# Decode attention on one Trainium2 core: 19 heads on VectorE, 13 on TensorE, wo of 24 heads and the MLP as one row, and wo of two heads by four DMA engines

## The chip, the cores and the metric

The kernel runs on one core of one Trainium2 chip. The metric is the device time of one execution in microseconds (us); lower is better. The first quotation for the kernel before is a median of 198.81 us over 3 runs (197.66 to 199.92). The profile is one execution; its span (196.6 us for the kernel before) leaves out about 2 us of start and end that the measured time includes.

In what follows PE is TensorE (matmuls), PEld its weight loads, DVE is VectorE, ACT is ScalarE, POOL is GpSimd and SP is SyncE, which issues most of the transfers.

## The reference, cut to what matters

One token of 512 features is normalised, attends with 32 heads to the last 4,096 of 32,768 cached positions, and is gated by an MLP.

```python
W = min(4096, max(256, Sk // 4))                       # 4096 of 32768
q = (xn @ wq) ...                                      # 32 heads x 128
scores = einsum("bhqd,bhkd->bhqk", q, k[:, :, Sk-W:]) * Dh**-0.5
o = einsum("bhqk,bhkd->bhqd", softmax(scores), v[:, :, Sk-W:])
s = o.reshape(B, Sq, Hq*Dh) @ wo                       # 4096 x 512
g = silu(B_ref(xn, w1, w2, w3, w4))                    # MLP, 512 -> 1376 -> 512
return x + s * g
```

The keys of one head in the window are 1 MB of bf16, the values too. With 64 such MB of keys and values, 4 MB each of wq and wo and the MLP weights, 78.85 million bytes have to come in.

## The kernel before: the parts that the argument touches

Transfers go out in one fixed order, on one queue: MLP weights, wq, the keys of head 0 to 4, then keys of head i and values of head i-5 in turn. There are 12 buffers for keys (wo of 8 heads takes one of them, three times) and 7 for values.

```python
def k_head(h, kn):                         # scores of one head
    ...
    if h % 2 == 0:                         # 16 heads on VectorE
        nc.vector.tensor_tensor(out=prod[:], in0=kn[:],
            in1=q_bc[:, h // 2:h // 2 + 1, :].to_broadcast([P, NC, Dh]), op=ALU.mult)
        nc.vector.tensor_reduce(out=s["sS"][:, hl // 2, :], in_=prod[:], axis=AX.X, op=ALU.add)
    else:                                  # 16 heads on TensorE, ScalarE copies
        for b in range(NB):
            for i in range(8):
                nc.tensor.transpose(pt[:, i, :], kn[:, b * 8 + i, :], ident_bf[:])
            nc.scalar.copy(out=kt[:, b * 8:(b + 1) * 8, :], in_=pt[:])
            if b == 0:
                flush()                    # matmuls of the head before
        pending.append((s["sT"], hl, h, kt))
    if hl == G - 1:                        # every 4th head
        softmax(g)                         # needs sS (VectorE) and sT (TensorE)

def rows_add(ps, col, w, last):            # "narrow": 4 matmuls of 128 columns,
    for j in range(KC):                    # accumulated in PSUM, no VectorE work
        nc.tensor.matmul(ps[32 * j:32 * j + 1, :], lhsT=col, rhs=w[0:k, j * P:(j + 1) * P],
                         start=False, stop=last, skip_group_check=True)

def apply_wo(i, ox):                       # wo of block i (8 heads), i = 0, 1, 2 and the few
    for t in range(8):
        rows_add(y_ps, ox[:, t:t + 1], wo_blk[i][:, t, :], False)
...
small.tile([P, 16], BF16, name="pad")      # decides where the later buffers lie
```

`oT` is the product of a head's probabilities `pT` with its values. After every 8 heads VectorE repacks the 8 outputs (`spread`, `pick`, `ox`), and TensorE applies that block of wo. wo of heads 24 to 31 is split: 2.5 heads (`wo_few`) are spread over the partitions so that five DMA engines carry them (in the trace each half of this load has five landings, a load of 128 partitions sixteen), the others come as rows at the end. After the last values come the last rows of wo, then `y = y_ps * g_row`, `out_row`, and the write of the output.

## Time and profile before

| kernel before | us | where it is read |
|---|---|---|
| median of 6 runs beside the changed kernel | 197.98 | the runs |
| span of the profiled run | 196.6 | the page |
| last group's softmax (`pT`) starts | 182.53 | ScalarE's row `pT<-e` |
| last values have landed | 191.60 | the chain of waits |
| `y` starts | 193.24 | the chain of waits |

The first profile line is the page's busy time by engine. After it comes VectorE's timeline around the third wo block: start and duration in us, engine, line, operation, output and inputs, shapes, count, and in brackets the idle time before the instruction and what ended it.

```profile
PE 125.2 (64%) x2448; PEld 112.3 (57%) x2448; DVE 129.5 (66%) x165; ACT 69.3 (35%) x82; POOL 6.3 (3%) x13
```

```profile
167.34 0.27 DVE L369 TENSOR_REDUCE ox<-pick 128x8 bf16<-128x64 f32 x1
169.34 2.29 DVE L274 TENSOR_TENSOR prod<-kv,q_bc 128x4096 bf16<-128x4096 bf16 x1 [1.74 <-DMA kv<-in_A_k_cache_dram]
171.67 4.42 DVE L277 TENSOR_REDUCE sS<-prod 128x32 f32<-128x4096 bf16 x1
176.12 0.22 DVE L296 TENSOR_REDUCE m<-sS 128x2 f32<-128x64 f32 x1
179.97 0.22 DVE L297 TENSOR_REDUCE m<-sT 128x2 f32<-128x64 f32 x1 [3.63 <-PE sT L255]
```

VectorE starts head 30 at 169.34, as soon as its keys are there, while TensorE is still at the third block of wo and at head 29. It has finished at 176.1 and then idles 3.63 us until TensorE has the scores of head 31. So here TensorE, not VectorE, sets the last softmax, and VectorE has idle time on both sides of head 30.

### The profile page before, as it was taken

To read this page: it belongs to the slowest core of one execution; us is meant where nothing else is said; L and a number is where in the kernel's file an instruction comes from. 1 tells how busy PE (TensorE), PEld (TensorE's weight loads), DVE (VectorE), ACT (ScalarE), POOL (GpSimd) and SP (SyncE) were. 2 spreads that over 40 slices of the span, in tenths; PEclk is the share of its full clock that TensorE was granted. 3 is DMA by queue.
4 is the path that set the end of the run, shared out by engine and by line. 5 is a ranking of instruction groups with operands and counts; after the bars stand their busy time and mean duration, and the time that the engine had idled before them with its cause. 6 is when DMAs were issued, how large, how long until landed. Compare 5 with 4: busy or idle time off the path is not lost.

```text
span 196.6 us, 5355 instructions
## 1 busy us (share of the span) xinstructions
PE 125.2 (64%) x2448; PEld 112.3 (57%) x2448; DVE 129.5 (66%) x165; ACT 69.3 (35%) x82; POOL 6.3 (3%) x13
## 2 busy tenths in 40 slices
PE   0564497646959683199565672399575930898563
PEld 0453335536949673199465662399574930897452
DVE  1530059998969988785497829693599479681401
ACT  2003028819445270076234340077170700455000
POOL 2110007000000000000000000000000000000000
PEclk9999999957675885557555555555566675555555
DMA  6999899999999999999999999999999999999970
GB/s 197 412 499 423 368 430 417 427 427 418 428 420 425 423 423 423 423 427 425 425 422 428 420 425 422 427 428 422 422 427 422 427 422 430 427 421 388 383 282 7
DMA packets 11480, 79.18 MB, mean 403 GB/s; under 512 B 1402, under 2 KB 2202, under 8 KB 2458
## 3 DMA queue, kind: packets, MB, share of 16 engines
q1 hardware_dynamic: 11306, 78.85, 96.4%
q8 instruction: 19, 0.31, 0.6%
q10 hardware_dynamic: 152, 0.00, 0.0%
q14 instruction: 3, 0.02, 0.0%
HBM read 78.84 MB, written 0.00 MB: 401 GB/s over the span
## 4 chain that ended last, share of the span: by engine, by line
DMA 91%; PE 5%; SPq 1%; issue 0%; DVE 0%
DMA kv<-in_A_v_cache_dram 41%; DMA kv<-in_A_k_cache_dram 31%; DMA wo<-in_A_wo_dram 10%; DMA wq_sb<-in_A_wq_dram 10%; PE qb_ps L234 3%; SPq L76 1%; PE qT_ps L225 1%; PE oT L402 1%; PE y_ps L139 0%; DVE y L454 0%; DVE out_row L456 0%
## 5 line engine op out<-in xcount | busy, mean ns | idle before, releaser
L284 ACT COPY kt<-pt 128x1024 bf16<-128x1024 bf16 x64 | 60.2, 1026 | 67.4 <-PE pt L283 67.4
L277 DVE TENSOR_REDUCE sS<-prod 128x32 f32<-128x4096 bf16 x16 | 70.6, 4415 | 0.3
L283 PE MATMUL pt<-ident_bf,kv 128*128 128x128 bf16 x512 | 53.0, 294 | 5.2 <-DMA kv<-in_A_k_cache_dram 4.5
L283 PEld LDWEIGHTS <-kv 128*128 128x128 bf16 x512 | 48.8, 138 | 6.8 <-DMA kv<-in_A_k_cache_dram 4.8
L274 DVE TENSOR_TENSOR prod<-kv,q_bc 128x4096 bf16<-128x4096 bf16 x16 | 36.6, 2285 | 7.5 <-DMA kv<-in_A_k_cache_dram 5.3
L402 PEld LDWEIGHTS <-kv 128*128 128x128 bf16 x1024 | 30.4, 102 | 16.3 <-issue 9.4
L402 PE MATMUL oT<-pT,kv 128*128 128x1 bf16 x1024 | 32.6, 165 | 8.0 <-DMA kv<-in_A_v_cache_dram 4.3
L255 PE MATMUL sT<-qT_bf,kt 128*128 128x1 bf16 x512 | 20.4, 166 | 3.8 <-ACT kt L284 3.4
L255 PEld LDWEIGHTS <-kt 128*128 128x128 bf16 x512 | 18.3, 103 | 4.8 <-ACT kt L284 4.6
L297 DVE TENSOR_REDUCE m<-sT 128x2 f32<-128x64 f32 x8 | 1.8, 224 | 18.4 <-PE sT L255 18.4
L139 PEld LDWEIGHTS <-ox 128*1 128x1 bf16 x96 | 2.2, 115 | 19.5 <-DVE ox L369 19.5
L363 PE MATMUL ox_ps<-spread,to 128*128 128x64 bf16 x4 | 0.8, 211 | 17.4 <-DVE spread L360 17.4
L316 ACT ACTIVATE pT<-e 128x128 bf16<-128x128 f32 x8 | 2.5, 310 | 20.4 <-DVE e L312 20.3
L307 PEld LDWEIGHTS mb_ps<-md,ones_f 4*128 4x128 f32 x16 | 3.5, 266 | 6.1 <-DVE md L304 6.1
L307 PE MATMUL mb_ps<-md,ones_f 4*128 4x4 f32 x16 | 4.2, 328 | 4.4 <-DVE md L304 4.4
L322 PE MATMUL den_ps<-pT,ones_bf 128*128 128x128 bf16 x8 | 2.1, 260 | 7.3 <-ACT pT L316 7.2
L234 PE MATMUL qb_ps<-wq_sb,xn_rep 128*128 128x512 bf16 x16 | 6.3, 578 | 0.0
L236 ACT CAST q_bc<-qb_ps 128x512 bf16<-128x512 f32 x4 | 2.3, 586 | 10.9 <-PE qb_ps L234 10.9
L300 PE MATMUL mt_ps<-ident_f,m 128*4 128x128 f32 x8 | 2.7, 335 | 4.8 <-DVE m L297 4.8
L405 DVE TENSOR_TENSOR o<-oT,rden 128x1 bf16<-128x1 f32 x4 | 0.6, 161 | 7.0 <-PE oT L402 7.0
L225 PE MATMUL qT_ps<-xn_bf,wq_sb 128*128 128x1 bf16 x64 | 1.9, 165 | 5.3 <-DMA wq_sb<-in_A_wq_dram 5.3
L225 PEld LDWEIGHTS <-wq_sb 128*128 128x128 bf16 x64 | 1.8, 104 | 5.6 <-DMA wq_sb<-in_A_wq_dram 5.6
(97 smaller groups left out, 63.3 us busy)
## 6 DMA issues: line engine op xcount, KB each, us to landing
kv<-in_A_k_cache_dram SPq DMA_DIRECT2D x32, 1024.0 KB, 19.6
kv<-in_A_v_cache_dram SPq DMA_DIRECT2D x32, 1024.0 KB, 19.6
wq_sb<-in_A_wq_dram SPq DMA_DIRECT2D x1, 4096.0 KB, 19.2
wo<-in_A_wo_dram SPq DMA_DIRECT2D x3, 1024.0 KB, 19.6
w_sb<-in_B_w_dram SPq DMA_DIRECT2D x1, 1376.0 KB, 6.7
w_sb<-in_B_w_dram SPq DMA_DIRECT2D x1, 1024.0 KB, 8.7
w_sb<-in_B_w_dram SPq DMA_DIRECT2D x1, 512.0 KB
wo_rows<-in_A_wo_dram SPq DMA_DIRECT2D x1, 384.0 KB, 15.9
```

The lines of the kernel that those rows point to most:

```text
L225: nc.tensor.matmul(qT_ps[:, h:h + 1], lhsT=wq_sb[:, c, h * Dh:(h + 1) * Dh], rhs=xn_bf[:, c:c + 1], start=(c == 0), stop=(c == KC - 1))
L234: nc.tensor.matmul(qb_ps[:], lhsT=xn_rep[:, c, :], rhs=wq_h[:, c, 2 * i:2 * i + 8:2, :], start=(c == 0), stop=(c == KC - 1))
L236: nc.scalar.copy(out=q_bc[:, i:i + 4, :], in_=qb_ps[:])
L255: nc.tensor.matmul(sT[:, hl // 2, c:c + 1], lhsT=kt[:, c, :], rhs=qT_bf[:, h:h + 1], start=True, stop=True)
L274: nc.vector.tensor_tensor(out=prod[:], in0=kn[:], in1=q_bc[:, h // 2:h // 2 + 1, :].to_broadcast([P, NC, Dh]), op=ALU.mult)
L277: nc.vector.tensor_reduce(out=s["sS"][:, hl // 2, :], in_=prod[:], axis=AX.X, op=ALU.add)
L283: nc.tensor.transpose(pt[:, i, :], kn[:, b * 8 + i, :], ident_bf[:])
L284: nc.scalar.copy(out=kt[:, b * 8:(b + 1) * 8, :], in_=pt[:])
L300: nc.tensor.transpose(mt_ps[:], m1[:].rearrange("p a b -> p (a b)"), ident_f[:])
L307: nc.tensor.matmul(mb_ps[:], lhsT=ones_f[0:G, :], rhs=md[:], start=True, stop=True)
L316: nc.scalar.activation(out=pT[:], in_=e[:], func=ACT.Exp, scale=scale)
L402: nc.tensor.matmul(oT[:, k:k + 1], lhsT=v[:, c, :], rhs=s["pT"][:, hl % 2, hl // 2, c:c + 1], start=(c == 0), stop=(c == NC - 1))
```

## The change

Its intent is to give TensorE and ScalarE less to do, to shorten the program, and to even out the DMA engines at the end. Three more heads (5, 13, 21) go to VectorE. wo of the first 24 heads and the MLP's output are computed "wide", as one row of 512 columns with one matmul instead of four; VectorE then takes the row out of PSUM and adds it to a running row. `wo_few` shrinks to 2 heads on four engines, and wo of two further heads is loaded ahead of the last values instead of earlier.

```diff
+MORE = (1, 3, 5)                 # groups in which VectorE takes three of four heads
-NE = 5
+NE = 4
-    small.tile([P, 16], BF16, name="pad")
+    small.tile([P, 32], BF16, name="pad")
...                               # MLP: 15 matmuls of 512 columns into hr_ps, copied to hr,
+    rows_add(h2_ps, one_f, hr, True)
...
-        if h % 2 == 0:
+        on_v, on_t = map(at, places(g))
+        if hl in on_v:
...
+    y_row = small.tile([1, D], FP32, name="y_row")
     def apply_wo(i, ox):
+        if i == few_block:
+            for t in range(8):
+                rows_add(y_ps, ox[:, t:t + 1], wo_blk[i][:, t, :], False)
+            return
+        yr_ps = ps_misc.tile([1, D], FP32, tag="misc", name="yr_ps")
         for t in range(8):
-            rows_add(y_ps, ox[:, t:t + 1], wo_blk[i][:, t, :], False)
+            nc.tensor.matmul(yr_ps[:], lhsT=ox[:, t:t + 1], rhs=wo_blk[i][:, t, :], start=(t == 0),
+                             stop=(t == 7))
+        if i == 0:
+            nc.vector.tensor_copy(out=y_row[:], in_=yr_ps[:])
+        else:
+            nc.vector.tensor_tensor(out=y_row[:], in0=y_row[:], in1=yr_ps[:], op=ALU.add)
+        if i == few_block - 1:
+            rows_add(y_ps, one_f, y_row, False)
...
+            if h == H - 1:
+                load_rows(h_part, H - G - h_part)
             v = load_kv(v_pool, A_v_cache, h)
...
-    for h in range(H - G, H):
+    for h in range(h_part, H):
         apply_rows(h)
```

Cut are the indexing that follows from 19 heads (`q_at`, `places`, the order inside a group) and the memsets.

More of the change, by code (lines that the diff above doesn't have):

```diff
@@ L106 @@
     nc.vector.memset(ones_f[:], 1.0)
+    one_f = ones_f[0:1, 0:1]
     ones_bf = const.tile([P, P], BF16, name="ones_bf")
@@ L172 @@
     nc.vector.tensor_copy(out=xn_bf[:], in_=xn_f[:])
-    xn_rep = small.tile([P, KC, P], BF16, name="xn_rep")
+    xn_rep = wts.tile([P, KC, P], BF16, name="xn_rep")
     nc.vector.tensor_copy(out=xn_rep[:], in_=xn_bf[:].unsqueeze(2).to_broadcast([P, KC, P]))
@@ L189 @@
     nc.vector.tensor_scalar(out=z3_bf[:], in0=xc3[:], scalar1=rstd3[:], scalar2=None, op0=ALU.mult)
-    hsr_ps = ps_misc.tile([P, P], FP32, tag="misc", name="hsr_ps")
-    rows_open(hsr_ps)
-    for c in range(KC):
-        rows_add(hsr_ps, shifted_bf[:, c:c + 1], w2_sb[:, c, :], c == KC - 1)
-    x1_row = small.tile([P, P], FP32, name="x1_row")
-    nc.vector.tensor_scalar(out=x1_row[:], in0=x_row[:], scalar1=negmean[:], scalar2=rstd[:],
+    xn_row = small.tile([P, P], FP32, name="xn_row")
+    nc.vector.tensor_scalar(out=xn_row[:], in0=x_row[:], scalar1=negmean[:], scalar2=rstd[:],
                             op0=ALU.add, op1=ALU.mult)
-    nc.vector.tensor_tensor(out=x1_row[:], in0=x1_row[:], in1=hsr_ps[:], op=ALU.add)
     chunks = [(P, slice(r, 8 * P, 8)) for r in range(8)]
@@ L210 @@
     nc.scalar.activation(out=a_bf[0:96, 10:11], in_=a_ps[0:96, 10:11], func=ACT.Gelu_apprx_tanh)
+    hr_ps = ps_misc.tile([1, D], FP32, tag="misc", name="hr_ps")
+    for c in range(KC):
+        nc.tensor.matmul(hr_ps[:], lhsT=shifted_bf[:, c:c + 1], rhs=w2_sb[:, c, :], start=(c == 0),
+                         stop=False)
+    for i, (m, _) in enumerate(chunks):
+        nc.tensor.matmul(hr_ps[:], lhsT=a_bf[0:m, i:i + 1], rhs=w4_sb[0:m, i, :], start=False,
+                         stop=(i == len(chunks) - 1))
@@ L211 @@
+    hr = wts.tile([1, D], FP32, name="hr")
+    nc.vector.tensor_copy(out=hr[:], in_=hr_ps[:])
     h2_ps = ps_misc.tile([P, P], FP32, tag="misc", name="h2_ps")
     rows_open(h2_ps)
-    for i, (m, _) in enumerate(chunks):
-        rows_add(h2_ps, a_bf[0:m, i:i + 1], w4_sb[:, i, :], i == len(chunks) - 1)
+    rows_add(h2_ps, one_f, hr, True)
     bv = small.tile([P, P], FP32, name="bv")
-    nc.vector.tensor_tensor(out=bv[:], in0=x1_row[:], in1=h2_ps[:], op=ALU.add)
+    nc.vector.tensor_tensor(out=bv[:], in0=xn_row[:], in1=h2_ps[:], op=ALU.add)
@@ L217, with places, at @@
     g_row = small.tile([P, P], FP32, name="g_row")
     nc.scalar.activation(out=g_row[:], in_=bv[:], func=ACT.Silu)
-    qT_ps = ps_misc.tile([P, H], FP32, tag="misc", name="qT_ps")
-    for h in range(1, H, 2):
+    def places(g):
+        if g in MORE:
+            return slice(0, G - 1, 1), slice(G - 1, G, 1)
+        return slice(0, G, 2), slice(1, G, 2)
+    def at(sl):
+        return list(range(G)[sl])
+    ve_runs = [range(8 * i, 8 * i + 8, 2) for i in range(H // 8)]
+    ve_runs += [range(G * MORE[0] + 1, G * MORE[-1] + 2, G * (MORE[1] - MORE[0]))]
@@ L224 @@
+    ve_heads = [h for r in ve_runs for h in r]
+    pe_heads = [h for h in range(H) if h not in ve_heads]
+    assert sorted(ve_heads) == [G * g + i for g in range(H // G) for i in at(places(g)[0])]
+    q_at = {h: i for hs in (ve_heads, pe_heads) for i, h in enumerate(hs)}
+    qT_ps = ps_misc.tile([P, len(pe_heads)], FP32, tag="misc", name="qT_ps")
+    for i, h in enumerate(pe_heads):
         for c in range(KC):
-            nc.tensor.matmul(qT_ps[:, h:h + 1], lhsT=wq_sb[:, c, h * Dh:(h + 1) * Dh],
+            nc.tensor.matmul(qT_ps[:, i:i + 1], lhsT=wq_sb[:, c, h * Dh:(h + 1) * Dh],
@@ L226 @@
                              rhs=xn_bf[:, c:c + 1], start=(c == 0), stop=(c == KC - 1))
-    qT_bf = small.tile([P, H], BF16, name="qT_bf")
-    nc.vector.tensor_copy(out=qT_bf[:, 1::2], in_=qT_ps[:, 1::2])
-    q_bc = small.tile([P, H // 2, Dh], BF16, name="q_bc")
+    qT_bf = small.tile([P, len(pe_heads)], BF16, name="qT_bf")
+    nc.vector.tensor_copy(out=qT_bf[:], in_=qT_ps[:])
+    q_bc = small.tile([P, len(ve_heads), Dh], BF16, name="q_bc")
     wq_h = wq_sb[:].rearrange("p c (h d) -> p c h d", d=Dh)
-    for i in range(0, H // 2, 4):
-        qb_ps = ps_tr.tile([P, 4, Dh], FP32, tag="pt", name="qb_ps")
+    for r in ve_runs:
+        n = len(r)
+        qb_ps = ps_tr.tile([P, n, Dh], FP32, tag="pt", name="qb_ps")
@@ L233 @@
         for c in range(KC):
-            nc.tensor.matmul(qb_ps[:], lhsT=xn_rep[:, c, :], rhs=wq_h[:, c, 2 * i:2 * i + 8:2, :],
+            nc.tensor.matmul(qb_ps[:], lhsT=xn_rep[:, c, :], rhs=wq_h[:, c, r[0]:r[-1] + 1:r.step, :],
                              start=(c == 0), stop=(c == KC - 1))
-        nc.scalar.copy(out=q_bc[:, i:i + 4, :], in_=qb_ps[:])
+        nc.scalar.copy(out=q_bc[:, q_at[r[0]]:q_at[r[0]] + n, :], in_=qb_ps[:])
     make_masks(8)
@@ L251, with qk @@
     rows_open(y_ps)
-    def qk(sT, hl, h, kt):
+    def qk(sT, i, h, kt):
         for c in range(NC):
-            nc.tensor.matmul(sT[:, hl // 2, c:c + 1], lhsT=kt[:, c, :], rhs=qT_bf[:, h:h + 1],
+            nc.tensor.matmul(sT[:, i, c:c + 1], lhsT=kt[:, c, :], rhs=qT_bf[:, q_at[h]:q_at[h] + 1],
                              start=True, stop=True)
@@ L268, in k_head @@
                 "sT": ps_s.tile([P, G // 2, NC], FP32, tag="sT", name="sT"),
-                "sS": sm_pool.tile([P, G // 2, NC], FP32, tag="sS", name="sS"),
+                "sS": sm_pool.tile([P, G - 1, NC], FP32, tag="sS", name="sS"),
             }
         s = st[g]
-        if h % 2 == 0:
+        on_v, on_t = map(at, places(g))
+        if hl in on_v:
             prod = prod_pool.tile([P, NC, Dh], BF16, tag="prod", name="prod")
             nc.vector.tensor_tensor(out=prod[:], in0=kn[:],
-                                    in1=q_bc[:, h // 2:h // 2 + 1, :].to_broadcast([P, NC, Dh]),
+                                    in1=q_bc[:, q_at[h]:q_at[h] + 1, :].to_broadcast([P, NC, Dh]),
                                     op=ALU.mult)
-            nc.vector.tensor_reduce(out=s["sS"][:, hl // 2, :], in_=prod[:], axis=AX.X, op=ALU.add)
+            nc.vector.tensor_reduce(out=s["sS"][:, on_v.index(hl), :], in_=prod[:], axis=AX.X, op=ALU.add)
         else:
@@ L286, in k_head @@
                     flush()
-            pending.append((s["sT"], hl, h, kt))
+            pending.append((s["sT"], on_t.index(hl), h, kt))
             if hl == G - 1:
@@ L294, in softmax @@
         s = st[g]
-        m1 = sm_pool.tile([P, 2, G // 2], FP32, tag="m1", name="m1")
-        nc.vector.tensor_reduce(out=m1[:, 0, :], in_=s["sS"][:], axis=AX.X, op=ALU.max)
-        nc.vector.tensor_reduce(out=m1[:, 1, :], in_=s["sT"][:], axis=AX.X, op=ALU.max)
+        parts = [(pl, len(at(pl)), src[:, 0:len(at(pl)), :])
+                 for pl, src in zip(places(g), (s["sS"], s["sT"]))]
+        m1 = sm_pool.tile([P, G], FP32, tag="m1", name="m1")
+        for pl, n, src in parts:
+            nc.vector.tensor_reduce(out=m1[:, pl], in_=src, axis=AX.X, op=ALU.max)
         mt_ps = ps_misc.tile([G, P], FP32, tag="misc", name="mt_ps")
-        nc.tensor.transpose(mt_ps[:], m1[:].rearrange("p a b -> p (a b)"), ident_f[:])
+        nc.tensor.transpose(mt_ps[:], m1[:], ident_f[:])
         mx = sm_pool.tile([G, 1], FP32, tag="mx", name="mx")
@@ L305, in softmax @@
                                 op0=ALU.mult)
-        mb_ps = ps_misc.tile([P, 2, G // 2], FP32, tag="misc", name="mb_ps")
+        mb_ps = ps_misc.tile([P, G], FP32, tag="misc", name="mb_ps")
         nc.tensor.matmul(mb_ps[:], lhsT=ones_f[0:G, :], rhs=md[:], start=True, stop=True)
-        mb = sm_pool.tile([P, 2, G // 2], FP32, tag="mb", name="mb")
+        mb = sm_pool.tile([P, G], FP32, tag="mb", name="mb")
         nc.vector.tensor_copy(out=mb[:], in_=mb_ps[:])
-        e = sm_pool.tile([P, 2, G // 2, NC], FP32, tag="e", name="e")
-        for i, src in enumerate((s["sS"], s["sT"])):
-            nc.vector.tensor_tensor(out=e[:, i], in0=src[:],
-                                    in1=mb[:, i, :].unsqueeze(2).to_broadcast([P, G // 2, NC]),
+        e = sm_pool.tile([P, G, NC], FP32, tag="e", name="e")
+        for pl, n, src in parts:
+            nc.vector.tensor_tensor(out=e[:, pl, :], in0=src,
+                                    in1=mb[:, pl].unsqueeze(2).to_broadcast([P, n, NC]),
                                     op=ALU.subtract)
-        pT = sm_pool.tile([P, 2, G // 2, NC], BF16, tag="pT", name="pT")
+        pT = sm_pool.tile([P, G, NC], BF16, tag="pT", name="pT")
         nc.scalar.activation(out=pT[:], in_=e[:], func=ACT.Exp, scale=scale)
@@ L332 @@
     FEW = 8 * 8 * NE
-    h_part, r_part = divmod(24 * P + FEW, P)
-    assert h_part + 1 < H - G and 0 < r_part < P and r_part % 32 == 0
+    h_part = 8 * few_block + FEW // P
+    assert FEW % P == 0 and h_part < H - G
     o_blk, wo_blk = {}, {}
@@ L398, in v_head @@
                 nc.vector.memset(o_blk[i][:], 0.0)
-        k = 2 * (hl % 2) + hl // 2
         oT, o = s["oT"], o_blk[i]
         for c in range(NC):
-            nc.tensor.matmul(oT[:, k:k + 1], lhsT=v[:, c, :], rhs=s["pT"][:, hl % 2, hl // 2, c:c + 1],
+            nc.tensor.matmul(oT[:, hl:hl + 1], lhsT=v[:, c, :], rhs=s["pT"][:, hl, c:c + 1],
                              start=(c == 0), stop=(c == NC - 1))
         if h >= H - G:
-            nc.vector.tensor_tensor(out=o[:, h % 8:h % 8 + 1], in0=oT[:, k:k + 1],
-                                    in1=s["rden"][:, k:k + 1], op=ALU.mult)
+            nc.vector.tensor_tensor(out=o[:, h % 8:h % 8 + 1], in0=oT[:, hl:hl + 1],
+                                    in1=s["rden"][:, hl:hl + 1], op=ALU.mult)
         elif hl == G - 1:
-            nc.vector.tensor_tensor(
-                out=o[:, h % 8 - 3:h % 8 + 1].rearrange("p (a b) -> p b a", b=2),
-                in0=oT[:].rearrange("p (b a) -> p b a", b=2),
-                in1=s["rden"][:].rearrange("p (b a) -> p b a", b=2), op=ALU.mult)
+            nc.vector.tensor_tensor(out=o[:, h % 8 - 3:h % 8 + 1], in0=oT[:], in1=s["rden"][:],
+                                    op=ALU.mult)
         ready, later[:] = later[:], []
@@ L419, in step @@
                 later.append(lambda: apply_wo(i, ox))
-                if i == few_block:
-                    later.append(lambda: [apply_rows(h) for h in range(h_part, H - G)])
             later.append(step)
@@ L434 @@
             wo_rows = v_pool.tile([P, H - h_part, D], BF16, tag="wo_rows", bufs=1, name="wo_rows")
-            nc.gpsimd.memset(wo_rows[0:r_part, 0, :], 0.0)
         if i >= LAG:
             h = i - LAG
+            if h == H - 1:
+                load_rows(h_part, H - G - h_part)
             v = load_kv(v_pool, A_v_cache, h)
@@ L442 @@
                 load_few()
-            if h == H - G - 1:
-                load(wo_rows[r_part:, 0, :], A_wo[h_part * P + r_part:(h_part + 1) * P, :])
-                load_rows(h_part + 1, H - G - h_part - 1)
             if h == H - 1:
```

## The prediction

> **What bounds the kernel now.** I read the page first: the slices, the queues, the shares of the chain.
>
> ```profile
> DMA  6999899999999999999999999999999999999970
> GB/s 197 412 499 423 368 430 417 427 427 418 428 420 425 423 423 423 423 427 425 425 422 428 420 425 422 427 428 422 422 427 422 427 422 430 427 421 388 383 282 7
> ...
> q1 hardware_dynamic: 11306, 78.85, 96.4%
> q8 instruction: 19, 0.31, 0.6%
> ...
> DMA 91%; PE 5%; SPq 1%; issue 0%; DVE 0%
> ```
>
> The DMA engines are full in every slice up to the last three, at some 424 GB/s. No compute engine is near that (the page gives VectorE 66%, TensorE 64%, ScalarE 35%). 91% of the chain of waits is transfers, and the 78.85 MB have to come in under either kernel. So engine work counts only in two places: where the DMA engines stop being full, and after the last value has landed. The table by windows and the chain in order of time show both:
>
> ```profile
> core 0: us, PE busy (x) PEld busy (x) DVE busy (x) ACT busy (x) POOL busy (x), PEclk, DMA share, GB/s
> ...
> 160.00:170.00 10.00, 3.65 (x80) 3.16 (x80) 7.92 (x9) 0.33 (x2) 0.00 (x0) 0.50 1.01 427
> 170.00:180.00 10.00, 9.94 (x213) 9.85 (x211) 6.30 (x4) 7.26 (x8) 0.00 (x0) 0.50 1.01 410
> 180.00:192.00 12.00, 7.42 (x187) 5.77 (x188) 3.21 (x16) 0.31 (x1) 0.00 (x0) 0.50 0.88 333
> ```
>
> ```profile
> 174.28 17.32 DMA kv<-in_A_v_cache_dram
> 191.60 0.05 issue
> 191.65 1.01 PE oT L402 x32
> 192.66 0.56 PE y_ps L139 x15
> 193.21 0.02 issue
> 193.24 0.30 DVE y L454
> ```
>
> From 180 to 192 us the rate is 333 instead of 424 GB/s: 12 us x 91 GB/s is 1.1 MB, or 2.6 us of full-rate transfer, lost. The last values (head 31) land at 191.60, and the span ends 4.98 us later, at 196.58.
>
> Why is it lost? The trace records, for each transfer, when each DMA engine finished its share. For the values of head 31 (us):
>
> ```
> 186.78 186.96 187.02 189.29 189.32 189.83 189.93 189.96 190.03 190.06 190.07 190.12 190.17 190.42 191.36 191.60
> ```
>
> Three engines are done 4.6 to 4.8 us before the last; the mean is 189.56. Perfect balance would be worth 2.0 us. Following the same record back shows how the lag arises. At 22.5 us one engine is 1.5 us behind, just after the first of the 19 instruction blocks (19.4 us); by 96 us the first eight blocks have put eight different engines 1.5 us behind. The ninth (98.0 us) hits one of these again: the slowest engine jumps from 0.0 to 1.45 us beyond the others. So the blocks seem to go round the same eight engines. Blocks 17, 18 and 19 (178.0, 187.4 and 190.9 us) begin a third round, and these are the stragglers at 191.36 and 191.60.
>
> [...]19 records of 16,384 bytes for 2,448 matmuls and 2,448 weight loads[...]. [...]each half of wo_few (5 rows of groups into 20 partitions) has five landings, every 128-partition transfer sixteen. [...]
>
> **The change part by part.** The costs come from these rows:
>
> ```profile
> L284 ACT COPY kt<-pt 128x1024 bf16<-128x1024 bf16 x64 | 60.2, 1026 | 67.4 <-PE pt L283 67.4
> L277 DVE TENSOR_REDUCE sS<-prod 128x32 f32<-128x4096 bf16 x16 | 70.6, 4415 | 0.3
> L283 PE MATMUL pt<-ident_bf,kv 128*128 128x128 bf16 x512 | 53.0, 294 | 5.2 <-DMA kv<-in_A_k_cache_dram 4.5
> ...
> L274 DVE TENSOR_TENSOR prod<-kv,q_bc 128x4096 bf16<-128x4096 bf16 x16 | 36.6, 2285 | 7.5 <-DMA kv<-in_A_k_cache_dram 5.3
> ```
>
> (1) Three heads (5, 13, 21) move from TensorE to VectorE. VectorE: 3 x (2.285 + 4.415) = +20.1 us, 129.5 to about 150, hidden if it stays within its buffers. Following VectorE's rows I get groups 1, 3 and 5 done at about 64, 102 and 140 us. The values of group 1 block the value load issued at 76.8 us (seven buffers), those of group 3 the load at 120, those of group 5 the load at about 159: 12 to 19 us to spare. TensorE loses 3 x 64 matmuls.
>
> (2) Wide rows. MLP: 16 + 44 matmuls become 15 with 512 columns plus four in fp32. wo of 24 heads: 3 x 32 become 3 x 8 plus four in fp32 (each fp32 matmul counts twice: the trace has 16 for 8). Busy time rises, since 512 columns took 0.43 us apiece in the q rows, but this lies beside transfers. The q part grows by a fifth group, about 1.2 us, and the MLP ends near 22 us, just as wq lands. The first value load then goes out at 32 to 33 us instead of 30.57; the keys already in flight last until 37.4, so no gap.
>
> (3) Instruction count. 2,448 matmuls less 192 (three heads), 8 (q), 37 (MLP) and 64 (wo), with small terms: 2,146, so 4,292 with weight loads. Block 17 was fetched before when 4,328 had begun. So only 16 are fetched: exactly two rounds, and no engine gets a third.
>
> (4) wo_few: 2 heads over four engines instead of 2.5 over five. The extra per chosen engine stays 64 KB: 8 packets x 0.309 us = 2.47 us. The fifth engine loses it, and half a head more is spread over all: 4 KB each, +0.15 us. The bytes ahead of the last values stay 512 KB.
>
> (5) End: 24 row matmuls instead of 16 after the last values, 8 x 0.60 / 16 = +0.30 us if none is done ahead.
>
> Sum: the slowest engine's lag is 4.8 us now. With two blocks it is 3.1 to 3.4, and a chosen engine that also had one of the smaller delays in the record gets to 3.6. That is -1.2 to -1.4; with +0.15 the last values land at about 190.5 us (-1.1). With +0.0 to +0.3 at the end the span is some 195.6, so **197.7 us** for the measured time (198.81 - 1.1, the end taken as mostly hidden).
>
> **Rivals.** (a) A new wait takes the gain. The values of head 28 are first used at 183.69, 0.96 us of which TensorE waited for the transfer:
>
> ```profile
> 182.53 0.31 ACT L316 ACTIVATE pT<-e 128x128 bf16<-128x128 f32 x1 [3.02 <-DVE e L312]
> ...
> 183.69 0.93 PEld L402 LDWEIGHTS <-kv 128*128 128x128 bf16 x32 [0.96 <-DMA kv<-in_A_v_cache_dram]
> 183.69 1.01 PE L402 MATMUL oT<-pT,kv 128*128 128x1 bf16 x32 [0.53 <-DVE rden L326]
> ```
>
> The last group's softmax is thus only about 1 us early. The third wide row costs 8 x 0.43 = 3.4 us on TensorE near 168 us and then needs a VectorE addition before TensorE goes on; behind a reduction that is up to 4.4 us. If it pushes the last softmax by over 3 us, the 1.6 us that TensorE idles before head 31 don't cover it: 198.5 to 200. I give it one in four. (b) VectorE becomes the bound: about 150 us of some 170 in which it has keys; a stall of the value buffers would lower the rate mid-span and give 200 to 203. The 12 us to spare speak against it: one in twenty. (c) Nothing moves, because a few-engine or another delay takes the straggler's place: 198.5 to 199. (d) Better balance still, and a faster TensorE clock at the end: 196, where 2.0 us of imbalance is the ceiling.
>
> **Range and chances.** The runs of before spread over 2.3 us, so noise is as large as the gain. (d) gives the low end, 196.0; (a) and (c) the high one, 199.3. Over 2% faster needs 194.8, beyond perfect balance: 0.04. Over 2% slower (202.8) needs (b): 0.03.
>
> **What would show it.** 16 instruction packets on q8 instead of 19; about 2,146 matmuls; four landings for each half of wo_few; the last values' landings spread over some 3.5 us instead of 4.8; the last values near 190.5 us; VectorE near 150 us with DMA share at 1.01 in all windows to 180 us. The prediction is wrong if a 17th block is fetched, if TensorE reaches head 31 later than its landing, or if the blocks go to other engines than the eight.

## The result, and the profile after

The changed kernel took **205.04 us** (median of 6 runs, 203.51 to 205.70), the kernel before 197.98 us beside it. The ratio is 1.033 with a 95% interval of 1.028 to 1.039: slower by over 2%. A ratio here is the mean time of one kernel's runs over that of the other's of the same rounds, so it is not quite the ratio of the medians quoted. The predicted 197.7 us and the range to 199.3 missed it.

From the page of the changed kernel: busy time, DMA share in 40 slices, the queue of instruction blocks, and the shares of the chain of waits.

```profile
PE 121.1 (60%) x2146; PEld 99.8 (49%) x2146; DVE 150.8 (74%) x174; ACT 58.6 (29%) x71; POOL 5.8 (3%) x12
...
DMA  6999999999999999999999999999999999999600
...
q8 instruction: 17, 0.28, 0.6%
...
DVE 57%; PE 26%; issue 10%; ACT 2%; DMA 2%; POOL 1%; DVEq 0%; ACTq 0%; POOLq 0%
```

The counts came as predicted: 2,146 matmuls, VectorE at 150.8 us. The DMA engines are as full as before, but they are done two slices before the end. The chain has turned over: transfers had 91% of it, now they have 2% and VectorE has 57%. The busy shares alone, 74% for the busiest engine, would not have told.

Where does VectorE lose time, if it is idle for a quarter of the span? The table by windows of the changed kernel (us; busy time and instructions of PE, PEld, DVE, ACT and POOL; granted TensorE clock; DMA share; GB/s) and VectorE's timeline of the same stretch:

```profile
170.00:175.00 5.00, 2.19 (x7) 0.53 (x7) 2.63 (x6) 0.00 (x0) 0.00 (x0) 0.50 1.02 424
175.00:180.00 5.00, 5.00 (x58) 3.79 (x56) 0.00 (x0) 3.83 (x4) 0.00 (x0) 0.62 1.02 424
```

```profile
172.70 0.27 DVE L394 TENSOR_REDUCE ox<-pick 128x8 bf16<-128x64 f32 x1
180.73 0.68 DVE L419 TENSOR_TENSOR y_row<-y_row,yr_ps 1x512 f32<-1x512 f32 x1 [7.77 <-PE yr_ps L414]
181.34 2.27 DVE L297 TENSOR_TENSOR prod<-kv,q_bc 128x4096 bf16<-128x4096 bf16 x1
183.64 4.42 DVE L300 TENSOR_REDUCE sS<-prod 128x32 f32<-128x4096 bf16 x1
```

Between 175 and 180 us VectorE does nothing at all. The keys of head 30 have been there since about 171 us, but the addition of the third wide row stands ahead of head 30 in VectorE's fixed order, and it waits 7.77 us for TensorE. The two earlier rows wait 1.47 and 1.46 us (at 91.1 and 133.8 us). TensorE's timeline shows why the third one waits so long:

```profile
173.02 1.87 PE L414 MATMUL yr_ps<-wo,ox 128*1 128x512 bf16 x4 [0.62 <-DVE ox L394]
174.82 2.74 PE L306 MATMUL pt<-ident_bf,kv 128*128 128x128 bf16 x24
177.49 0.58 PE L414 MATMUL yr_ps<-wo,ox 128*1 128x512 bf16 x1
178.01 0.97 PE L306 MATMUL pt<-ident_bf,kv 128*128 128x128 bf16 x8
178.91 0.59 PE L414 MATMUL yr_ps<-wo,ox 128*1 128x512 bf16 x2
179.43 0.95 PE L441 MATMUL oT<-pT,kv 128*128 128x1 bf16 x32
180.32 0.38 PE L414 MATMUL yr_ps<-wo,ox 128*1 128x512 bf16 x1
```

The source writes the eight wide matmuls in one loop, but they are not issued in one go: in the built program the 32 transposes of head 29 and the values of head 24 stand between them. At 0.43 us apiece the row would have been done after 3.4 us; it takes from 173.02 to 180.7. The 3.4 us are my estimate: four of these matmuls took 1.87 us and one by itself 0.58, so each further one 0.43 us, (1.87 - 0.58) / 3. The granted clock was 0.50 during all five of these and 1.00 during the last three of the row.

The end of the changed kernel, in order of time:

```profile
190.68 0.31 ACT L341 ACTIVATE pT<-e 128x128 bf16<-128x128 f32 x1 [2.97 <-DVE e L337]
...
197.40 1.00 PE L441 MATMUL oT<-pT,kv 128*128 128x1 bf16 x32
...
198.99 0.29 DVE L486 TENSOR_TENSOR y<-y_ps,g_row 128x128 f32<-128x128 f32 x1 [0.39 <-PE y_ps L141]
```

The last softmax comes at 190.68, 8.15 us later than before. The last values had landed at 191.79, almost as before (191.60), but TensorE came to them only at 197.40, with no wait for a transfer. `y` starts at 198.99, 8.31 us after the softmax. That is 5.75 us later than before. Another 0.85 us lies after it: from the issue of the output's write to its landing the changed kernel took 2.48 us (199.63 to 202.11) and the kernel before 1.63 us (193.88 to 195.51). In the changed kernel an instruction block of 8,192 bytes on another queue had been moved at 200.76, just ahead of the output's packets at 200.86. In e9 below such a block comes just ahead too (200.99 and 201.06), and the landing takes 2.58 us; in no other trace does one, and there it takes 1.62 to 1.64 us. That the block is the cause was not tested.

### The profile page after: what moved, and what is told of

It is laid out like the page before. It is cut to its first block, busy times and chain, and to the rows that moved or that the text cites. A ratio compares the mean times of both kernels' runs of the same rounds, so it can differ in the third digit from the quotient of the medians.

```text
span 203.1 us, 4749 instructions
## 1 busy us (share of the span) xinstructions
PE 121.1 (60%) x2146; PEld 99.8 (49%) x2146; DVE 150.8 (74%) x174; ACT 58.6 (29%) x71; POOL 5.8 (3%) x12
## 4 chain that ended last, share of the span: by engine, by line
DVE 57%; PE 26%; issue 10%; ACT 2%; DMA 2%; POOL 1%; DVEq 0%; ACTq 0%; POOLq 0%
DVE sS L300 31%; DVE prod L297 16%; PE yr_ps L414 5%; PE pt L306 5%; PE oT L441 5%; PE mb_ps L332 2%; DMA x_bf<-in_A_x_dram 2%; ACT kt L307 2%; PE hr_ps L214 1%; PE a_ps L203 1%; DVE m L322 1%; PE sT L277 1%; DVE e L337 1%; PE mt_ps L325 1%; DVE mx L327 1%
## 5 line engine op out<-in xcount | busy, mean ns | idle before, releaser
L300 DVE TENSOR_REDUCE sS<-prod 128x32 f32<-128x4096 bf16 x19 | 83.8, 4412 | 0.3
L307 ACT COPY kt<-pt 128x1024 bf16<-128x1024 bf16 x52 | 49.2, 1024 | 78.9 <-PE pt L306 78.9
L297 DVE TENSOR_TENSOR prod<-kv,q_bc 128x4096 bf16<-128x4096 bf16 x19 | 43.3, 2281 | 1.4 <-ACT q_bc L258 1.3
L306 PE MATMUL pt<-ident_bf,kv 128*128 128x128 bf16 x416 | 43.0, 294 | 0.7 <-ACT kt L307 0.5
L306 PEld LDWEIGHTS <-kv 128*128 128x128 bf16 x416 | 39.5, 138 | 2.8 <-issue 2.0
L441 PEld LDWEIGHTS <-kv 128*128 128x128 bf16 x1024 | 30.4, 102 | 14.4 <-issue 14.3
L277 PE MATMUL sT<-qT_bf,kt 128*128 128x1 bf16 x416 | 16.4, 165 | 3.2 <-ACT kt L307 2.9
L277 PEld LDWEIGHTS <-kt 128*128 128x128 bf16 x416 | 14.4, 101 | 4.5 <-ACT kt L307 4.0
L414 PE MATMUL yr_ps<-wo,ox 128*1 128x512 bf16 x24 | 10.6, 593 | 1.9 <-DVE ox L394 1.9
L419 DVE TENSOR_TENSOR y_row<-y_row,yr_ps 1x512 f32<-1x512 f32 x2 | 1.4, 676 | 9.2 <-PE yr_ps L414 9.2
L334 DVE COPY mb<-mb_ps 128x4 f32<-128x4 f32 x8 | 1.3, 159 | 4.7 <-PE mb_ps L332 4.7
```

Of the source, the lines that this page charges most:

```text
L277: nc.tensor.matmul(sT[:, i, c:c + 1], lhsT=kt[:, c, :], rhs=qT_bf[:, q_at[h]:q_at[h] + 1], start=True, stop=True)
L297: nc.vector.tensor_tensor(out=prod[:], in0=kn[:], in1=q_bc[:, q_at[h]:q_at[h] + 1, :].to_broadcast([P, NC, Dh]), op=ALU.mult)
L300: nc.vector.tensor_reduce(out=s["sS"][:, on_v.index(hl), :], in_=prod[:], axis=AX.X, op=ALU.add)
L414: nc.tensor.matmul(yr_ps[:], lhsT=ox[:, t:t + 1], rhs=wo_blk[i][:, t, :], start=(t == 0), stop=(t == 7))
L441: nc.tensor.matmul(oT[:, hl:hl + 1], lhsT=v[:, c, :], rhs=s["pT"][:, hl, c:c + 1], start=(c == 0), stop=(c == NC - 1))
```

## The experiments

The reading to test: **the end is the later of two chains**. One is the last values' landing plus the work after it; the other is the last softmax plus the work after it. The change pushes the second past the first, and the three things that can push it are the 19 heads, the wide rows, and VectorE's order. The rivals: VectorE's load alone (19 heads), TensorE's longer rows alone, transfers (later loads, another place in memory), or the MLP row. Each quoted expectation explains its own names for the theories. The kernel before was run again in each of the three groups of four runs, which ran on three chips: medians 198.03, 198.15 and 198.07 us.

A few times in each trace stand here in one table, in us. "Third block" is the start of TensorE's first matmul of the third wo block; "+" is from there to the last softmax; "landed" is the last values' landing. The times up to "`y` starts" are from one trace each. The kernel before and e5 are the same program: their third blocks differ by 0.45 us and their softmaxes by 0.31 us, so smaller differences than that say nothing.

| run | heads on VectorE | wide rows of wo | values start on a multiple of 256 bytes | third block | + | last softmax | landed | `y` starts | median | ratio to before (95%) |
|---|---|---|---|---|---|---|---|---|---|---|
| before | 16 | 0 | yes | 167.66 | 14.87 | 182.53 | 191.60 | 193.24 | 197.98 | |
| after | 19 | 3 | no | 173.02 | 17.66 | 190.68 | 191.79 | 198.99 | 205.04 | 1.033 (1.028-1.039) |
| e1 | 19 | 0 | no | 171.16 | 14.70 | 185.86 | 191.78 | 194.15 | 199.04 | 1.004 (1.002-1.006) |
| e2 | 16 | 3 | no | 169.60 | 16.83 | 186.43 | 192.99 | 194.74 | 199.96 | 1.009 (1.008-1.011) |
| e3 | 19 | 3, by ScalarE | no | 171.35 | 15.98 | 187.33 | 191.74 | 195.63 | 200.21 | 1.010 (1.007-1.014) |
| e4 | 19 | 0 | no | 170.72 | 14.87 | 185.59 | 191.91 | 194.07 | 199.53 | 1.007 (1.005-1.010) |
| e5 | 16 | 0 | yes | 168.11 | 14.73 | 182.84 | 191.43 | 193.06 | 198.77 | 1.004 (1.001-1.006) |
| e6 | 16 | 0 | no | 169.37 | 14.39 | 183.76 | 192.76 | 194.46 | 200.20 | 1.010 (1.009-1.012) |
| e7 | 16 | 3 | yes | 168.69 | 17.59 | 186.28 | 192.33 | 194.76 | 198.68 | 1.004 (1.000-1.008) |
| e8 | 16 | 0 | yes | 167.80 | 14.87 | 182.67 | 190.44 | 192.12 | 197.79 | 0.998 (0.996-1.000) |
| e9 | 19 | 3 | yes | 173.19 | 17.71 | 190.90 | 191.02 | 199.20 | 205.37 | 1.036 (1.033-1.038) |
| e10 | 19 | 2 | yes | 173.57 | 14.71 | 188.28 | 189.64 | 196.57 | 201.50 | 1.018 (1.012-1.023) |
| e11 | 16 | 0 | yes | 169.96 | 14.39 | 184.35 | 190.80 | 192.62 | 198.68 | 1.003 (0.997-1.010) |
| e12 | 19 | 0 | yes | 169.80 | 14.50 | 184.30 | 190.51 | 192.78 | 198.48 | 1.002 (0.998-1.006) |

**The two chains.** In every row `y` starts either 8.27 to 8.48 us after the last softmax or 1.63 to 1.70 us after the landing, whichever is later. Only before, e5, e6 and e8 follow the landing. The work after the softmax takes 8.48 us where wo is split as before (e4, e7, e12) and 8.27 to 8.31 us in the others that follow it. So the last softmax of the kernel before had 193.24 - (182.53 + 8.48) = 2.2 us to spare (1.7 us in e5, by the same sum), or 2.4 us counted with the changed kernel's 8.31.

**e1, the changed kernel with wo of 24 heads narrow.**

```diff
+WIDE = ()
-        if i == few_block:
+        if i == few_block or i not in WIDE:
```

> The changed kernel with wo of the 24 heads applied as in the kernel before (3 x 32 narrow matmuls straight into the result, no addition on VectorE); 19 heads on VectorE stay. Theory 1 (VectorE stood 7.77 us waiting for the third wide row, ahead of the product of head 30): that wait is gone, the last softmax comes back to about 183 us, and the time to about 197.5 us (196.5 to 199). Theory 2 (19 heads make VectorE the bound, it simply runs late): nothing much changes, 203 to 205 us.

It took 199.04 us: 6 of the 7 us were gone, with 19 heads on VectorE and everything else of the change kept. The wide rows are thus a necessary part of the loss. The last softmax came back to 185.86 only, not to about 183, and the time is just above the expected range.

**e2, the changed kernel with 16 heads on each engine.**

```diff
-MORE = (1, 3, 5)
+MORE = ()
```

> The changed kernel with heads 5, 13 and 21 back on TensorE (16 and 16), all else as changed, wide rows included. Theory 1: VectorE still stands some 3.5 to 8 us at the third wide row, so 200 to 204 us. Theory 2: VectorE has 20 us less to do, so about 198 us.

It took 199.96 us, though its three row additions wait 7.21, 7.62 and 6.83 us, longer in sum than in the changed kernel. That is at the edge of theory 1 and 2 us above theory 2, but no more than the kernel before takes with its buffers in the same place (e6 below: 200.20 us). So the 19 heads are a necessary part too: with either of the two undone, most of the loss goes. The length of a wait is not its cost.

**e3, the changed kernel with ScalarE taking the rows out and TensorE adding them.**

```diff
-        if i == 0:
-            nc.vector.tensor_copy(out=y_row[:], in_=yr_ps[:])
-        else:
-            nc.vector.tensor_tensor(out=y_row[:], in0=y_row[:], in1=yr_ps[:], op=ALU.add)
-        if i == few_block - 1:
-            rows_add(y_ps, one_f, y_row, False)
+        nc.scalar.copy(out=y_row[:], in_=yr_ps[:])
+        rows_add(y_ps, one_f, y_row, False)
```

> The changed kernel with the wide rows of wo kept, but ScalarE copies each row out of the accumulator and TensorE adds it to the result, so VectorE never waits for it. VectorE keeps 19 heads. Theory 1: 196.5 to 199 us, VectorE idle for under 2 us between 165 and 181 us. Theory 2: 202 to 205 us.

The wide matmuls are all there, but VectorE doesn't wait for them: 200.21 us, over the range of theory 1 and far below that of theory 2. So nearly 5 us of the loss come from VectorE standing in line for the rows and taking them out (three operations of 0.68 us), not from the longer row on TensorE. What the wide row costs on TensorE itself shows in VectorE's wait for the scores of head 31, in this run and then in e12, which has narrow rows:

```profile
184.77 0.23 DVE L322 TENSOR_REDUCE m<-sT 128x2 f32<-128x64 f32 x1 [6.57 <-PE sT L277]
```

```profile
181.75 0.22 DVE L320 TENSOR_REDUCE m<-sT 128x2 f32<-128x64 f32 x1 [5.09 <-PE sT L275]
```

The wait is 6.57 us against 5.09, and from the third block to the softmax it is 15.98 us against 14.4 to 14.9 in all runs with a narrow third row: 1.1 to 1.6 us.

**e4, the kernel before with the 19 heads alone.** The edit is the change's hunks on `MORE`, `places` and `q_at`, with narrow rows, the old MLP and `NE = 5`. It kept the change's `pad` of 32.

```diff
+MORE = (1, 3, 5)
+WIDE = ()
-    small.tile([P, 16], BF16, name="pad")
+    small.tile([P, 32], BF16, name="pad")
```

> The kernel before with 19 heads on VectorE and 13 on TensorE and nothing else of the change (narrow rows for wo and the MLP, wo of 2.5 heads by five engines). Theory 1: 197 to 199 us, within noise of before, as the buffers hide the 20 us of VectorE work. Theory 2: 202 to 205 us.

199.53 us, so 0.7% over the kernel before and half a microsecond over what theory 1 had said. I could not explain it from VectorE's work alone, and comparing the DMA records showed something else: the mean time of an 8,192-byte transfer between 40 and 140 us was 314.37 ns against 310.49 ns before, in the changed kernel 314.19. In the built programs the value buffers had moved by 128 bytes. e6 tests that. As e1 also has the MLP row and the new balance, e1 against e4 (last softmax 185.86 and 185.59) shows that the MLP row does no harm there.

**e5, the kernel before, unaltered.** A control: how far do two identical kernels differ?

> The kernel before, unchanged, as a control for the next runs on the same chip. Question: every run after the first showed the 8,192-byte transfers at 314.3 ns apiece instead of 310.5 ns. Theory A (the chip of those runs is slower): this run shows 314 ns too. Theory B (the change's memory layout does it: the value buffers sit 128 bytes past a multiple of 256 in all those kernels, and on a multiple of 256 in the kernel before): this run shows 310.5 ns. The time is within 0.5% of before by construction.

198.77 us, a ratio of 1.0036 with an interval of 1.0009 to 1.0063 that does not contain 1. So a difference of 0.4% is not read as one, whatever its interval says. Its transfers took 310.42 ns, on another chip than e1 to e4, so the slower transfers of e1 to e4 are not their chip's (theory A).

**e6, the kernel before with its buffers moved by 128 bytes.** No instruction differs.

```diff
-    small.tile([P, 16], BF16, name="pad")
+    small.tile([P, 80], BF16, name="pad")
```

> The kernel before with a padding tile 128 bytes longer, so that the value, weight and wo buffers sit 128 bytes past a multiple of 256, as in the changed kernel; not one instruction differs. Theory A: same as before, within 0.3%. Theory B: 314.3 ns per 8,192-byte transfer and about 2 us more (1.0%), 199.5 to 200.5 us.

200.20 us, 1.0% over the kernel before and 0.7% over the control. The transfers took 314.37 ns each on average and the last values landed at 192.76 instead of 191.60. So the place of the buffers is a cost by itself, of about 1.2 us at the landing, and the changed kernel has it. Why is open: the keys lie at 128 bytes past a multiple of 256 in every one of these kernels, and in the kernel before they are moved as fast as the values (at least nine in ten of the 8,192-byte transfers between 40 and 140 us take 309 ns, and about half of those are keys), so it isn't a plain matter of one misaligned buffer.

**e7, the kernel before with the three wide rows alone.**

```diff
+WIDE = (0, 1, 2)
...                               # apply_wo as in the change, wide for i in WIDE
```

> The kernel before with the wide rows for wo of 24 heads and nothing else of the change (16 and 16 heads; value buffers on a multiple of 256). The row's wait: VectorE stands some 7 us at the third row, but with less behind it than in the changed kernel, so the last softmax ends near 185 us instead of 182.5 and the time is 198 to 200 us. If the wide row were harmless without 19 heads: 198.0 us, last softmax at 182.5.

198.68 us, no more than the control. Its rows wait 7.41, 6.59 and, here, 7.69 us:

```profile
176.33 0.68 DVE L395 TENSOR_TENSOR y_row<-y_row,yr_ps 1x512 f32<-1x512 f32 x1 [7.69 <-PE yr_ps L390]
```

The third block starts 1.03 us later than before (168.69 against 167.66), but most of that is no row's doing: this trace is late from VectorE's first product on, here of the kernel before and of e7:

```profile
26.79 2.29 DVE L274 TENSOR_TENSOR prod<-kv,q_bc 128x4096 bf16<-128x4096 bf16 x1 [2.17 <-ACT q_bc L236]
```

```profile
27.62 2.29 DVE L276 TENSOR_TENSOR prod<-kv,q_bc 128x4096 bf16<-128x4096 bf16 x1 [2.17 <-ACT q_bc L238]
```

Less these 0.83 us the first two rows cost 0.2 us, which is within what two traces of one kernel differ by. e2 against e6, which have the same place of the buffers and first products at the same time (26.95), says the same: 169.60 against 169.37, with the MLP row and the new balance in e2. The first two waits fell into time in which VectorE would have waited anyway: in sum it waits 3.6 us for TensorE's scores here and not at all for keys, against 18.4 and 5.3 us before. The third row adds 2.7 us after that (17.59 against 14.87). The sum, 3.75 us on the last softmax, is over the 2.2 us to spare, and `y` is 1.5 us later in this trace. It is the slowest of the four runs (200.08 us; the others 198.26 to 198.97), which fits its late start.

**e8, the kernel before with the new balance of wo alone** (`NE = 4`, the rows of two heads ahead of the last values).

```diff
-NE = 5
+NE = 4
...
+            if h == H - 1:
+                load_rows(h_part, H - G - h_part)
             v = load_kv(v_pool, A_v_cache, h)
```

> The kernel before with wo of two heads by four engines and of two more ahead of the last values, and nothing else. The prediction's model: the slowest engine still gets three instruction blocks, so the last values land at 191.6 +- 0.3 us and the time stays within 0.4% of before (197.5 to 198.8). Rival: the fifth engine's share or the moved rows matter, 1 us or more either way.

197.79 us, the fastest of all kernels here, with a ratio of 0.998. The margin is smaller than what the control shows, so I don't call it a gain. The last values landed at 190.44, 1.2 us earlier than before, though the spread between the DMA engines was 4.63 us, nearly the old one. I had expected 191.6, and what brought them earlier is open.

**e9, the changed kernel with its buffers on multiples of 256 bytes.**

```diff
-    small.tile([P, 32], BF16, name="pad")
+    small.tile([P, 96], BF16, name="pad")
```

> The changed kernel with its padding 128 bytes longer, so that the value, weight and wo buffers sit on a multiple of 256 again; no instruction differs. If the chain through VectorE sets its end (19 heads plus the wait for the third row), the faster transfers are hidden: 204 to 205.5 us, last softmax at 190 us or later. If the layout cost adds to the rest: 202 to 203.5 us.

The transfers were quick again (310.25 ns), and the time was 205.37 us: nothing gained. In the changed kernel the transfers are not what the end waits for, so the cost of e6 is hidden. The slower transfers are out as the cause of the loss.

**e10, e9 with the third row narrow.**

```diff
+WIDE = (0, 1)
-        if i == few_block:
+        if i == few_block or i not in WIDE:
```

> The changed kernel, buffers on a multiple of 256, with only the third block of wo (heads 16 to 23) applied by 32 narrow matmuls; the first two stay wide, 19 heads stay, the balance stays. Theory (only the third row's wait reaches the end, the first two are absorbed): last softmax near 185 us, values land near 190 us, time 197.5 to 199 us. Rival (any wide row costs, VectorE is late throughout): 201 us or more.

201.50 us. Removing the 7.8 us wait gained 3.9 us. I had expected the first two rows to be absorbed (197.5 to 199 us), and that was wrong: they cost as much again. VectorE's waits for them are 1.03 and 1.47 us, with two operations of 0.68 us, 3.86 us in sum, and the third block starts 3.77 us later than in e12 (173.57 against 169.80). Nothing was absorbed. The gain of the third row on the last softmax is only 2.6 us in these traces (190.90 to 188.28), and the reason is VectorE's wait for head 31 here:

```profile
180.21 0.22 DVE L323 TENSOR_REDUCE m<-sS 128x2 f32<-128x64 f32 x1
185.82 0.23 DVE L323 TENSOR_REDUCE m<-sT 128x2 f32<-128x64 f32 x1 [5.39 <-PE sT L278]
```

Without the wait of 7.8 us VectorE is done with head 30 eight microseconds earlier, and then waits 5.39 us for TensorE. In e9 that second wait is nil. The difference of the two waits, with the row's own 0.68 us, is about the 3.0 us by which "+" is longer in e9. Most of the rest of the 3.9 us lies after `y`: e9's output landed 2.58 us after its issue, as in the changed kernel, e10's 1.63 us after it.

**e11, the kernel before with wo of four heads meant for eight DMA engines.**

```diff
-NE = 5
+NE = 8
```

> The kernel before (16 and 16 heads, narrow rows) with wo of four heads, 24 to 27, loaded by eight engines, none ahead of the last values, and 16 row matmuls at the end as before. Model: the instruction blocks go round eight engines[...]: last values land near 190 us instead of 191.5, time 196.3 to 197.5 us, below both kernels. [...]

198.68 us with a wide interval: the 196.3 to 197.5 us that were expected did not come, and the run is inconclusive. The landing came at 190.80, 0.8 us earlier than before, but the spread grew to 5.33 us, and `y` followed the softmax (184.35 + 8.27) by then, so the earlier landing could not have been used in full. The third block is as late here (169.96) as in e12 below, but for another reason: VectorE starts head 30 at 171.30 after waiting 1.39 us for its keys (169.34 before), whereas e12 starts it at 169.66 with no such wait. What made the keys late is open. That the eight engines of this load are others than those of the instruction blocks was my assumption; it was not shown, and which engines the instruction blocks load could not be told from the run.

**e12, e4 with its values on a multiple of 256 bytes**, that is, 19 heads alone without the cost of e6.

```diff
-    small.tile([P, 32], BF16, name="pad")
+    small.tile([P, 96], BF16, name="pad")
```

> 19 heads on VectorE and nothing else of the change, value buffers on a multiple of 256 (the earlier run of this part had them 128 bytes off). Layout theory: the 1 to 2 us that the earlier run lost were the layout's, so 197.5 to 198.7 us here. If the 19 heads cost by themselves: 199 to 200 us.

198.48 us: 19 heads alone cost nothing that can be measured. e4's loss was the place of its buffers. But the trace shows what they used up: VectorE no longer waits for keys (5.3 us in sum before), and for TensorE's scores 5.9 us instead of 18.4, 5.1 of them at head 31. The last softmax is at 184.30, 1.8 us later than before, and `y` (192.78) already follows it; the landing would have allowed 190.51 + 1.64 = 192.15. The reserve is gone before any row is added.

**The sum.** In the kernels with values on multiples of 256 bytes the last softmax moves by 8.37 us from before to e9. The start of the third block moves by 2.14 us with 19 heads (e12) and by 5.53 us with the rows as well (e9). So the first two rows cost 3.4 us with 19 heads (3.8 us by e10; up to 0.4 us of it may be the MLP row and the new balance, by e1 against e4), and 0.2 us with 16: with 16 heads their waits lie in VectorE's idle time, with 19 heads there is no such time. The third row adds 2.84 us (17.71 against 14.87). 5.53 + 2.84 = 8.37; less the 2.4 us to spare, 5.97, and `y` moved by 5.96. That last agreement is no proof of its own, as the 2.4 us come from the same two traces. With the buffers where the change has them the parts are others: the third block moves by 1.7 us with the place (e6), 1.4 us with 19 heads (e4), 0.4 us with the MLP row and the balance (e1) and 1.9 us with two rows (after), and the third row adds 3.0 us (after against e1). The shares depend on the order in which the parts are added; the whole does not.

## Why the prediction was wrong, by its own steps

**What bounds the kernel before: right, but not measured out.** Transfers do, and the end follows them. The prediction read the last softmax as "only about 1 us early", from the wait of one instruction. The experiments give about 2 us to spare (2.2 or 2.4, as counted above). More important, no step of the prediction added up what the parts of the change together would take from it.

**Step (1), the 19 heads: the step that failed first.** The load was right (150.8 us for "about 150"). "Hidden if it stays within its buffers" asked when the values' buffers come free, with "12 to 19 us to spare", and that was the wrong test. The heads alone are indeed hidden (e12), but they take VectorE's idle time in mid-span. In the kernel before VectorE waits 5.3 us in sum for keys and 18.4 us for TensorE's scores; in e12 it waits 0 and 5.9 us. That idle time was what every later row needed, and the last softmax moved 1.8 us before any row.

**Step (2), the wide rows: wrong for wo.** "This lies beside transfers" counted only TensorE's busy time. It left out that the row leaves PSUM on VectorE, in the program's order, ahead of the next head's product: an operation of 0.68 us, after waits of 1.47, 1.46 and 7.77 us in the changed kernel. The first two rows cost 3.4 us with 19 heads and 0.2 us with 16 (e9 against e12; e7 against before, and e2 against e6). For the MLP the step held within 0.4 us (e1 against e4), though the first value load went out at 27.6 us and not at 32 to 33.

**Rival (a): the right mechanism with too small a size and chance.** It named this wait: the third row, then a VectorE addition, pushing the last softmax. It gave 3.4 us for the row plus up to 4.4 behind a reduction. The wait was 7.77 us, for another reason: TensorE did a head's transposes and another's values between the row's matmuls. Of it 2.8 us reached the softmax, as VectorE would otherwise have waited later for head 31. So the third row's share was about as sized; the 5.5 us that had already come before it, from step (1), step (2) and both together, made the difference between some 199 and 205 us.

**Rival (b), VectorE as the bound: half right.** It was given one in twenty and looked for a stall of the value buffers and a lower transfer rate in mid-span. The rate stayed at 424 GB/s (170 to 180 us) and there was no such stall. VectorE became the bound in another way, through the order of its own instructions to the last softmax.

**Step (3), the instruction count: matmuls exact, blocks off by one.** 2,146 matmuls as said, but 17 blocks of 16,384 bytes instead of 16; the last is fetched at 199.97, after `y`, so it does not reach the result by itself. A 17th block was one of the prediction's own signs of being wrong; why it is fetched is open. The spread of the last landings was 3.7 us, close to the 3.5 that was named, against 4.8 before: in all traces with 15 or 16 blocks before the landing it is 3.7 to 4.0 us, with 18 or 19 it is 4.6 to 5.3. In the kernel before one engine ended wq at 22.49 us, the 15 others by 20.99, after the first block at 19.4 us. No run changed the blocks alone. So less lag came, but it could not pay, as the end no longer followed the landing.

**Step (4), wo_few: right in what it counted.** There are four landings for each half. e8, which has this and the rows alone, is at 197.79, what the whole change had been predicted to be, but that is luck: the prediction drew its gain from fewer blocks, and e8 still fetches 19.

**The landing: 191.79 instead of 190.5.** The buffers' place was missed, and it costs some 1.2 us (e6), which is nearly the whole difference; with it put right the landing is 191.02 (e9) and 189.64 (e10). The last values' load also goes out at 180.42 us instead of 174.28, as its buffer comes free only when TensorE has used the values of head 24, which stood behind the wide row (the line at 179.43 above). No cost of that shows: the first engine is done with its share of that load at 188.09, and a share is eight packets of 0.31 us, about 2.5 us, so even this engine came to it only at about 185.6 (my estimate from the trace). Here are the changed kernel's issues:

```profile
171.17 0.39 SPq L77 DMA_DIRECT2D wo_rows<-in_A_wo_dram  x1
180.42 0.33 SPq L77 DMA_DIRECT2D kv<-in_A_v_cache_dram  x1
```

**Step (5), the end: right to a few tenths, and beside the point.** The work from the last softmax on is 8.3 us in the new order and 8.5 in the old.

**What would show it.** The prediction named as its own refutation "if TensorE reaches head 31 later than its landing". That is what the trace shows: 197.40 against 191.79. So does the 17th block.

Open are the effect of 128 bytes on the transfers, the earlier landing in e8, the 0.85 us at the output's write, and which DMA engines the instruction blocks load. None of them carries the 5.75 us by which `y` moved.

## What to carry to other kernels

Where transfers bound a kernel, as here with 91% of the chain of waits, first measure how much later the other chain, here the last softmax and the work after it, may come (1.7 to 2.4 us here); then add up what all parts of a change take from that one reserve, for each part alone may fit (1.002, 1.004 and 0.998 here) and the whole not (1.033). VectorE, at 66%, had its idle time spread between fixed instructions, and that time took up waits: 19 heads alone (76%) brought its waits for keys and for TensorE's scores from 5.3 and 18.4 us to 0 and 5.9 while the time stayed the same (198.48 us), and only with those heads did the rows show in the time (205.37 us in e9; 198.68 with 16 heads, e7). Before a result is handed to another engine, look at what stands behind it in that engine's order (here head 30, behind a wait of 7.77 us) and at what the producer will do in between (here the transposes of one head and the values of another, so that the row took 7.7 us and not the 3.4 of the estimate); a wait's cost is what is left of it after the next wait, here 2.84 of about 7.8 us (e9).
